# Attention ahead of two routed layers: the order of the background work, of two subtractions and of the q loads

## The chip, the cores and the metric

The kernel runs on one core of a Trainium2 chip. The time is device microseconds of one execution. The kernel before took 952.51 us as the median of three runs (949.66 to 957.09). One further execution was recorded by the hardware profiler; it took 954.63 us, and its span from the first to the last instruction is 952.9 us.

## The reference

Attention over 8 batches, 8 heads, 576 positions and 64 features, with K and V averaged over groups of 8 positions (72 pooled rows). Its output is 4608 tokens of 512 features. They pass a layer of 8 experts (each token goes to one), and then a second such layer with a skip gate.

```python
k_p = k.reshape(B, H, Sp, pool, D).mean(axis=3)
v_p = v.reshape(B, H, Sp, pool, D).mean(axis=3)
scores = scale * np.matmul(q, k_p.transpose(0, 1, 3, 2))
attn = softmax(scores)                       # maximum subtracted first
x = np.matmul(attn, v_p)                     # tokens: (B*S, H*D) = (4608, 512)
# layer 1: top-1 of 8 experts, chosen by logits = x @ w_gate + bias[modality]
out[mask] = gate_w[mask, None] * (np.maximum(x[mask] @ w1[e], 0) @ w2[e])
# layer 2: only rows with x @ w_skip > 0; top-1 again; those rows get x + y
y[mask] = np.maximum(xc[mask] @ w1[e], 0) @ w2[e]
```

## The kernel before

**Attention** works through 36 columns of 128 tokens (c = 0 to 35, `NC`), software-pipelined over three columns (`LAG` = 3). In one turn of the loop at L565, `emit_S` (L299) multiplies scores into the PSUM tile `ps_s` (L310), VectorE (DVE) takes their maximum `mx` (L316), and what stands in the list `late` follows on DVE. `emit_eT` turns the exponentials of the column before (L357), `emit_exp` subtracts the maximum by a matmul (L336, which waits for `mx`) and ScalarE (ACT) takes the exponential `ec` (L340). `emit_AV` (L364) multiplies the column three back with V (L377), and the generator `after_AV` divides on DVE: `rec` (L398, L400), `lg` (L402), `x` (L405), and in the next column the logits `LG` (L409). The finished x goes out to `xd` through SyncE's queue SP (L417, L423).

**Loads and preparation.** SP issues every load in program order. `next_q` loads a unit of q (256 tokens, `q_sb`, L141), `next_kv` the raw K and V (`kt` L121, `v` L132). Eight rows are added by GpSimd (POOL) in a tree of three additions, `pool_rows` (L181 to L183), or by one DVE reduction (L176). `split_q` copies q on ACT (`qs`, L167), `prep_k` transposes the sums (L239) and copies them on ACT into `KB` (L244), `prep_v1` transposes V's sums (L255).

**Background.** The routing of layer 1 starts within attention. Its steps are generators in a queue; `bg.tick()` takes `bg.pace` steps of the first one. `route` finds each token's expert and its rank by a scan (`rt_i` L868, `carry` L872, two matmuls into `R` at L883 and L884) for columns 0 to 8, 9 to 17, 18 to 26 (from c = 12, 21, 30) and 27 to 35 (after the loop). `route_places` writes, per column, two 128x128 tables `OB` (L912) on POOL, for the third group on POOL and DVE in turn. `early_pick` chooses the expert that is worked on first: `count` rounds `carry` into `rc_cb` (L920), multiplies it by ones into `R` (L924), and `er_most`, `er_s` follow (L955, L957). `early_fill` counts a second time for block 1, `early_places` works out `er_oa` (L1013), and `early_slots` turns `er_oa` and `OB` into row numbers by 54 small matmuls into `W0` (L1028) and `rs_lo`, `rs_v` on DVE (L1047, L1049).

**Start of layer 1.** From c = 30 `prepare_first` splits the first weights into a high part (`w1h`, ACT) and a low part (`w1l`, DVE, L1328); at c = 32 and 33 it transposes the gathered tokens into `ps_x` (L1356) and splits these too (`xh` ACT, `xl` DVE, L1360). From c = 35 `gemm1_early` runs one of eight parts f0 to f7 of the first GEMM-1 (L1408, 12 matmuls each; `hh` on ACT L1412, `hl` on DVE L1413), and behind f7 GEMM-2 (L1461) opens the layers proper, which take the rest of the span.

The PSUM tiles `ps_k`, `ps_v`, `ps_g` (attention), `R`, `W0` and `ps_x` share one single buffer (`ps_m`): each waits until the reader of the one before it is done. While `bg.hold` is set, whoever wants that buffer first runs the background on until the flag is cleared (`bg.settle`).

Of the kernel before, what the change touches and what calls it, by code (L numbers as in the profile page):

```python
# [9 lines left out]
F32 = mybir.dt.float32  # L10
# [45 lines left out]
def attention(tc, g, q, k, v, mid, w_gate, bias, const, moe):  # L56
# [4 lines left out]
    with ExitStack() as ctx:  # L61
# [243 lines left out]
        def emit_S(c, then=lambda: None):  # L305
# [18 lines left out]
            next(av)  # L324
            bg.tick()
            bg.tick()
            s_t[c] = ps, mx, av
# [38 lines left out]
        def emit_AV(c):  # L366
# [14 lines left out]
            av = av_t[c] = after_AV(c, ps)  # L381
            next(av)
            bg.tick()
            next(av)
            bg.tick()
            next(av)

# [177 lines left out]
        for c in range(NC + LAG):  # L565
            if c < NC:
                next_q(cols[c][0] + (5 if c == 2 else 4))
                next_kv(c)
                next_q(cols[c][0] + 5)
            if c in (22, 32, 36):  # L570
                bg.pace = 1 if c == 32 else 2
            if 4 <= c < NC - 1:
                emit_S(c, lambda: emit_qT(c + 2))
            elif c < 4:
                if c > 0:
                    emit_S(c)
                    emit_eT(c - 1)
                    emit_exp(c)
                emit_qT(c + 2)
            elif c == NC - 1:  # L580
                emit_S(c, moe.gemm1_early)
            if 4 <= c < NC:
# [40 lines left out]
            if c in route_at:  # L623
# [4 lines left out]
                if c0 == 9:  # L628
                    bg.add(early_places(tc, g, g.r1, 18, 0, 2, sm))
                bg.add(route_places(tc, g, g.r1, c0, n, nc.gpsimd, nc.vector if c0 == 18 else None))  # L630
                if c0 == 18:
                    bg.add(early_fill(tc, g, g.r1, 512, sm, ps_m))
                    bg.add(early_places(tc, g, g.r1, 27, 2, 2, sm))
                    bg.add(early_slots(tc, g, g.r1, 27, g.r1.gidx0[:, 2:4], sm, ps_m))
                    bg.add(moe.gather_second())
# [7 lines left out]
            if c == NC - 3:  # L643
                qs.close()
                moe.open_second()
            moe.prepare_first(c, sm, ps_q, ps_m)
        for _ in av_t.pop(NC - 1):
# [268 lines left out]

def count(tc, g, r, sp, pp, wait):
    nc = tc.nc
# [5 lines left out]
    nc.tensor.matmul(N, lhsT=g.ones, rhs=cb, start=True, stop=True)  # L924
    g.bg.hold = True
    for _ in range(wait):
# [21 lines left out]
def early_pick(tc, g, r, sp, pp, wait=4, fill=None):  # L948

    V = tc.nc.vector  # L950
    N = yield from count(tc, g, r, sp, pp, wait)
    most = sp.tile([128, 1], F32, tag="er_most", name="er_most", bufs=1)
# [17 lines left out]
def early_fill(tc, g, r, n, sp, pp, wait=4):  # L970
    V = tc.nc.vector
    N = yield from count(tc, g, r, sp, pp, wait)
    s = sp.tile([128, E], F32, tag="er_s", name="er_s", bufs=1)
# [203 lines left out]
class Moe:  # L1177
# [146 lines left out]

    def split_w1(self, f, eng=None):
        raw = self.w1r[f // 2][:, :, 128 * (f % 2):128 * (f % 2) + 128]
        self.nc.scalar.copy(self.w1h[f], raw)  # L1327
        (eng or self.nc.vector).tensor_tensor(self.w1l[f], raw, self.w1h[f].bitcast(F32),  # L1328
                                              ALU.subtract)

# [21 lines left out]

    def xT(self, i, t, ps):
        nc = self.nc
        for k in range(4):
# [3 lines left out]
        nc.scalar.copy(hi, ps)  # L1359
        nc.vector.tensor_tensor(self.xl[i % 2][:, :, 128 * t:128 * t + 128], ps, hi.bitcast(F32),  # L1360
                                ALU.subtract)

# [123 lines left out]

    def prepare_first(self, c, sm, ps_q, ps_m):
        self.ps_q = ps_q
        for f in {30: (0,), 31: (1,), 32: (2,), 33: (3,), 34: (4,), 35: (5,), 36: (6,), 37: (7,)}.get(c, ()):
            self.split_w1(f)  # L1490
        if c in (32, 33):
            self.g.bg.settle()
            self.xT(0, c - 32, ps_m.tile([128, 4, 128], F32, tag="m", name="ps_x"))
        if c == 36:
# [594 lines left out]
```

## Time and profile before

| | profiled execution |
|---|---|
| time, span | 954.63 us, 952.9 us |
| TensorE matmul (PE) | 897.7 us busy, 94% of the span |
| weight load (PEld) | 803.9 us, 84% |
| DVE | 689.6 us, 72% |
| POOL | 518.7 us, 54% |
| ACT | 373.4 us, 39% |
| mean granted TensorE clock | 0.978 |

PE is the engine that is busy nearly always, so what it waits for is what the span is made of. The granted clock is the share of the full 2.4 GHz that TensorE was given; at half of it a matmul takes twice as long. In the page's 40 slices PE is busy 8 or 9 tenths of each of the first nine, up to 214 us, and nearly always 9 beyond. Attention and the start of layer 1 fill the first 216 us; the change acts there.

### The profile page before, as it was taken

The numbers are of one execution on the slowest core, as the hardware profiler recorded it, in microseconds if no ns is written. First come the engines' busy times: TensorE is split into PE (matmuls) and PEld (weight loads), VectorE is DVE, ScalarE is ACT, GpSimd is POOL, SyncE is SP. The second block draws the span as 40 slices with busy tenths as digits, with TensorE's granted clock in tenths as the row PEclk, the third lists the DMA queues.
The fourth block names the chain that finished last, engine by engine and source line by source line (L and its number), as shares of the span: only waits on it lengthen the run. The fifth ranks groups of instructions, "written<-read, shape, count | busy, mean of one in ns | idle before, by whom it ended". The sixth has DMA issues, their size and how long they took to land. (4 is left out here: it accounts for less than half of the span.)

```text
span 952.9 us, 19141 instructions
## 1 busy us (share of the span) xinstructions
PE 897.7 (94%) x6239; PEld 803.9 (84%) x6239; DVE 689.6 (72%) x1826; ACT 373.4 (39%) x735; POOL 518.7 (54%) x766
## 2 busy tenths in 40 slices
PE   8899999889999999998999989999889999999994
PEld 6788888888899999996999879999778988979983
DVE  5477787776787788889877898877665667577564
ACT  3456565544122222242222422213403556565554
POOL 5764698404246647666766657575543443445443
PEclk9799999999999999999999999999989999999998
DMA  9999765513211212341224421227114673671441
GB/s 229 223 260 259 223 196 167 185 63 120 72 57 58 95 38 65 125 171 66 74 81 134 174 78 63 74 79 244 60 60 146 216 226 122 203 238 36 128 140 42
DMA packets 86136, 126.02 MB, mean 132 GB/s; under 512 B 13192, under 2 KB 50104, under 8 KB 85866
## 3 DMA queue, kind: packets, MB, share of 16 engines
q1 hardware_dynamic: 75386, 96.68, 32.8%
q0 software_dynamic: 10608, 27.67, 9.5%
q8 instruction: 62, 1.02, 0.4%
q14 instruction: 80, 0.66, 0.2%
HBM read 184.18 MB, written 39.50 MB: 235 GB/s over the span
## 5 line engine op out<-in xcount | busy, mean ns | idle before, releaser
L1408 PE MATMUL ps_g<-xh,w1h 128*128 128x256 f32 x896 | 255.9, 286 | 2.0 <-DVE g_su L1391 1.2
L1408 PE MATMUL ps_g<-xl,w1h 128*128 128x256 f32 x896 | 253.6, 283 | 2.2 <-DVE xl L1360 2.2
L1408 PE MATMUL ps_g<-xh,w1l 128*128 128x256 f32 x896 | 253.0, 282 | 0.0
L1742 DVE CUSTOM_DVE_ANT_0 junk<-x,W 128x512 bf16<-128x512 f32 x324 | 228.2, 704 | 18.7 <-DVEq L1338 6.3
L1461 PE MATMUL ps_g<-w2h,hl 128*128 128x512 f32 x464 | 185.4, 399 | 7.0 <-DVE hl L1413 7.0
L1461 PE MATMUL ps_g<-w2h,hh 128*128 128x512 f32 x464 | 191.1, 412 | 0.7 <-DVE rs_v L1049 0.5
L1461 PE MATMUL ps_g<-w2l,hh 128*128 128x512 f32 x464 | 184.4, 397 | 0.0
L1408 PEld LDWEIGHTS ps_g<-xh,w1h 128*128 128x128 f32 x896 | 170.0, 190 | 8.0 <-issue 1.6
L1408 PEld LDWEIGHTS ps_g<-xl,w1h 128*128 128x128 f32 x896 | 169.2, 189 | 3.9 <-DVE xl L1360 3.0
L1408 PEld LDWEIGHTS ps_g<-xh,w1l 128*128 128x128 f32 x896 | 169.2, 189 | 0.0
L1412 ACT ACTIVATE hh<-ps_g 128x512 fp32r<-128x512 f32 (+1 forms) x116 | 67.6, 583 | 245.6 <-PE ps_g L1408 238.7
L912 POOL TENSOR_SCALAR OB<-iota,BB,pay 128x128 bf16<-128x128 bf16 x126 | 110.7, 887 | 22.4 <-DVE BB L900 19.0
L1413 DVE SCALAR_TENSOR_TENSOR hl<-ps_g,hh 128x512 fp32r<-128x512 f32 (+1 forms) x116 | 77.6, 669 | 62.0 <-ACT hh L1412 35.5
L1461 PEld LDWEIGHTS ps_g<-w2h,hl 128*128 128x128 f32 x464 | 88.0, 190 | 30.5 <-DVE hl L1413 8.3
L1461 PEld LDWEIGHTS ps_g<-w2h,hh 128*128 128x128 f32 x464 | 88.3, 190 | 20.5 <-issue 1.9
L1461 PEld LDWEIGHTS ps_g<-w2l,hh 128*128 128x128 f32 x464 | 88.4, 190 | 16.6
L1328 POOL TENSOR_TENSOR w1l<-w1r,w1h 128x512 fp32r<-128x512 f32 x39 | 50.5, 1314 | 63.1 <-ACT w1h L1327 62.8
L1350 DVE TENSOR_TENSOR w2l<-w2r,w2h 128x512 fp32r<-128x512 f32 x112 | 74.9, 706 | 8.2 <-ACT w2h L1349 4.8
L1708 POOL DMA_INDIRECT out_dram<-x,dsi x38 | 48.1, 1265 | 44.7 <-ACTq L1343 11.6
L1327 ACT CAST w1h<-w1r 128x512 fp32r<-128x512 f32 x120 | 68.3, 620 | 0.4 <-ACT hh L1412 0.4
L1349 ACT CAST w2h<-w2r 128x512 fp32r<-128x512 f32 x112 | 63.9, 616 | 4.0 <-DVE gidxf L1052 2.5
L1320 POOL DMA_INDIRECT xg<-xd,gidx x38 | 45.1, 1188 | 32.8 <-DVE rs_lo L1171 15.7
(295 smaller groups left out, 1393.9 us busy)
## 6 DMA issues: line engine op xcount, KB each, us to landing
w1r<-in_moe_w_dram SPq DMA_DIRECT2D x128, 512.0 KB
w2r<-in_moe_w_dram SPq DMA_DIRECT2D x128, 512.0 KB
x2s<-x SPq DMA_DIRECT2D x19, 522.0 KB
v<-in_v_dram SPq DMA_DIRECT2D x48, 192.0 KB
xd<-x SPq DMA_DIRECT2D x16, 520.0 KB
q_sb<-in_q_dram SPq DMA_DIRECT2D x16, 512.0 KB
kt<-in_k_dram SPq DMA_DIRECT2D x32, 144.0 KB
x2s<-OBx SPq DMA_DIRECT2D x16, 261.0 KB
```

The costliest lines, as they stand in the source:

```text
L912: e.tensor_scalar(g.ob(c)[:, i, :], g.iota, r.BB[:, c:c + 1], r.pay[:, i, c:c + 1], ALU.is_equal, ALU.mult)
L1320: self.nc.gpsimd.indirect_dma_start(out=self.xg[i % 2][:, t, 0:w], out_offset=None, in_=src, in_offset=bass.IndirectOffsetOnAxis(ap=gidx[: ...
L1327: self.nc.scalar.copy(self.w1h[f], raw)
L1328: (eng or self.nc.vector).tensor_tensor(self.w1l[f], raw, self.w1h[f].bitcast(F32), ALU.subtract)
L1349: self.nc.scalar.copy(self.w2h[f], raw)
L1350: (eng or self.nc.vector).tensor_tensor(self.w2l[f], raw, self.w2h[f].bitcast(F32), ALU.subtract)
L1408: nc.tensor.matmul(out, lhsT=a[f][:, k, :], rhs=b[:, k, :], start=(n == 0), stop=(n == 11))
L1412: nc.scalar.activation(out=hh, in_=whole, func=ACTF.Relu)
L1413: nc.vector.scalar_tensor_tensor(hl, in0=whole, scalar=0.0, in1=hh.bitcast(F32), op0=ALU.max, op1=ALU.subtract)
L1461: nc.tensor.matmul(ps, lhsT=a[f][:, tt], rhs=b[f], start=(n == 0), stop=(n == 23))
L1708: self.nc.gpsimd.indirect_dma_start(out=self.out, out_offset=bass.IndirectOffsetOnAxis(ap=self.dsi[i % 2][:, t:t + 1], axis=0), in_=self.x ...
L1742: self.nc.vector.tensor_tensor_reduce(out=self.junk, in0=self.x2[i % 2][:, t, 0:DM], in1=self.W9[:, e, :], scale=1.0, scalar=0.0, op0=ALU. ...
```

## The change

Seven edits, all to the order of things; no arithmetic is added or removed, but for three small copies:

1. `emit_AV` takes no background steps between the divisions of its column; `emit_S` takes four behind the maximum instead of two (with the one after `emit_exp` and the one ahead of the AV steps it is six per column as before).
2. From c = 2 on, q is loaded five units ahead (before: four, and five at c = 2), so that its load stands ahead of the column's K and V in SP's queue.
3. At c = 35 the first part of GEMM-1 is emitted behind all of `emit_S`, where it stood between the scores and the maximum.
4. The pace of the background is 2 at c = 34 and 35 and 3 from c = 36 (before: 1 and 2).
5. The third group's `route_places` runs in turn with `early_fill` and `early_places`, where these came behind it.
6. In `early_pick` and `early_fill` ACT copies the count out of PSUM (`rc_N`), and the background is not held.
7. The subtractions `w1l` (c = 30 to 34) and `xl` (c = 32, 33) go into `late`, that is behind the maximum of the next column.

```diff
@@ -322,8 +322,8 @@
             bg.tick()
             av = av_t.pop(c - LAG - 1, idle())
             next(av)
-            bg.tick()
-            bg.tick()
+            for _ in range(4):
+                bg.tick()
             s_t[c] = ps, mx, av
 
         late = []
@@ -379,11 +379,8 @@
                                      rhs=VB[b % NR][:, j].rearrange("p i w -> p (i w)"),
                                      start=(j % 3 == 0), stop=(j % 3 == 2), skip_group_check=True)
             av = av_t[c] = after_AV(c, ps)
-            next(av)
-            bg.tick()
-            next(av)
-            bg.tick()
-            next(av)
+            for _ in range(3):
+                next(av)
 
         def after_AV(c, ps):
             u, r = cols[c]
@@ -564,11 +561,10 @@
         route_at = {12: (0, 9), 21: (9, 9), 30: (18, 9)}
         for c in range(NC + LAG):
             if c < NC:
-                next_q(cols[c][0] + (5 if c == 2 else 4))
+                next_q(cols[c][0] + (5 if c > 1 else 4))
                 next_kv(c)
                 next_q(cols[c][0] + 5)
-            if c in (22, 32, 36):
-                bg.pace = 1 if c == 32 else 2
+            bg.pace = {22: 2, 32: 1, 34: 2, 36: 3}.get(c, bg.pace)
             if 4 <= c < NC - 1:
                 emit_S(c, lambda: emit_qT(c + 2))
             elif c < 4:
@@ -578,7 +574,8 @@
                     emit_exp(c)
                 emit_qT(c + 2)
             elif c == NC - 1:
-                emit_S(c, moe.gemm1_early)
+                emit_S(c)
+                moe.gemm1_early()
             if 4 <= c < NC:
                 emit_eT(c - 1)
                 emit_exp(c)
@@ -627,10 +624,12 @@
                              early_pick(tc, g, g.r1, sm, ps_m, 7) if c0 == 9 else (), lag))
                 if c0 == 9:
                     bg.add(early_places(tc, g, g.r1, 18, 0, 2, sm))
-                bg.add(route_places(tc, g, g.r1, c0, n, nc.gpsimd, nc.vector if c0 == 18 else None))
+                places = route_places(tc, g, g.r1, c0, n, nc.gpsimd, nc.vector if c0 == 18 else None)
+                if c0 < 18:
+                    bg.add(places)
                 if c0 == 18:
-                    bg.add(early_fill(tc, g, g.r1, 512, sm, ps_m))
-                    bg.add(early_places(tc, g, g.r1, 27, 2, 2, sm))
+                    bg.add(together(places, chain(early_fill(tc, g, g.r1, 512, sm, ps_m),
+                                                  early_places(tc, g, g.r1, 27, 2, 2, sm))))
                     bg.add(early_slots(tc, g, g.r1, 27, g.r1.gidx0[:, 2:4], sm, ps_m))
                     bg.add(moe.gather_second())
             if c == 27:
@@ -643,7 +642,7 @@
             if c == NC - 3:
                 qs.close()
                 moe.open_second()
-            moe.prepare_first(c, sm, ps_q, ps_m)
+            moe.prepare_first(c, sm, ps_q, ps_m, late if c < NC - 1 else None)
         for _ in av_t.pop(NC - 1):
             pass
         g.pm.pool = ps_m
@@ -914,7 +913,7 @@
         yield
 
 
-def count(tc, g, r, sp, pp, wait):
+def count(tc, g, r, sp, pp, wait, copy=False):
     nc = tc.nc
     cb = sp.tile([128, E], BF16, tag="rc_cb", name="rc_cb", bufs=1)
     nc.vector.tensor_copy(cb, r.carry)
@@ -922,7 +921,11 @@
         yield
     N = pp.tile([128, E], F32, tag="m", name="R")
     nc.tensor.matmul(N, lhsT=g.ones, rhs=cb, start=True, stop=True)
-    g.bg.hold = True
+    if copy:
+        ps, N = N, sp.tile([128, E], F32, tag="rc_N", name="rc_N", bufs=1)
+        nc.scalar.copy(N, ps)
+    else:
+        g.bg.hold = True
     for _ in range(wait):
         yield
     return N
@@ -948,7 +951,7 @@
 def early_pick(tc, g, r, sp, pp, wait=4, fill=None):
 
     V = tc.nc.vector
-    N = yield from count(tc, g, r, sp, pp, wait)
+    N = yield from count(tc, g, r, sp, pp, wait, True)
     most = sp.tile([128, 1], F32, tag="er_most", name="er_most", bufs=1)
     mx = sp.tile([128, 1], F32, tag="er_mx", name="er_mx", bufs=1)
     s = sp.tile([128, E], F32, tag="er_s", name="er_s", bufs=1)
@@ -969,7 +972,7 @@
 
 def early_fill(tc, g, r, n, sp, pp, wait=4):
     V = tc.nc.vector
-    N = yield from count(tc, g, r, sp, pp, wait)
+    N = yield from count(tc, g, r, sp, pp, wait, True)
     s = sp.tile([128, E], F32, tag="er_s", name="er_s", bufs=1)
     f = sp.tile([128, 1], F32, tag="er_most", name="er_most", bufs=1)
     V.tensor_tensor(s, N, r.star, ALU.mult)
@@ -1322,11 +1325,12 @@
                 in_offset=bass.IndirectOffsetOnAxis(ap=gidx[:, c + t:c + t + 1], axis=0),
                 bounds_check=src.shape[0] - 1, oob_is_err=False)
 
-    def split_w1(self, f, eng=None):
+    def split_w1(self, f, eng=None, late=None):
         raw = self.w1r[f // 2][:, :, 128 * (f % 2):128 * (f % 2) + 128]
         self.nc.scalar.copy(self.w1h[f], raw)
-        (eng or self.nc.vector).tensor_tensor(self.w1l[f], raw, self.w1h[f].bitcast(F32),
-                                              ALU.subtract)
+        low = partial((eng or self.nc.vector).tensor_tensor, self.w1l[f], raw,
+                      self.w1h[f].bitcast(F32), ALU.subtract)
+        low() if late is None else late.append(low)
 
     def load_split(self, i):
         ET = mybir.EngineType
@@ -1350,15 +1354,16 @@
         (eng or self.nc.vector).tensor_tensor(self.w2l[f], raw, self.w2h[f].bitcast(F32),
                                               ALU.subtract)
 
-    def xT(self, i, t, ps):
+    def xT(self, i, t, ps, late=None):
         nc = self.nc
         for k in range(4):
             nc.tensor.transpose(ps[:, k, :], self.xg[i % 2][:, t, 128 * k:128 * k + 128],
                                 self.g.ident)
         hi = self.xh[i % 2][:, :, 128 * t:128 * t + 128]
         nc.scalar.copy(hi, ps)
-        nc.vector.tensor_tensor(self.xl[i % 2][:, :, 128 * t:128 * t + 128], ps, hi.bitcast(F32),
-                                ALU.subtract)
+        low = partial(nc.vector.tensor_tensor, self.xl[i % 2][:, :, 128 * t:128 * t + 128], ps,
+                      hi.bitcast(F32), ALU.subtract)
+        low() if late is None else late.append(low)
 
     def ps_t(self, name):
         return self.pp.tile([128, 4, 128], F32, tag="tp", name=name, bufs=2)
@@ -1484,13 +1489,13 @@
         self.gathered = True
         yield
 
-    def prepare_first(self, c, sm, ps_q, ps_m):
+    def prepare_first(self, c, sm, ps_q, ps_m, late):
         self.ps_q = ps_q
         for f in {30: (0,), 31: (1,), 32: (2,), 33: (3,), 34: (4,), 35: (5,), 36: (6,), 37: (7,)}.get(c, ()):
-            self.split_w1(f)
+            self.split_w1(f, late=late)
         if c in (32, 33):
             self.g.bg.settle()
-            self.xT(0, c - 32, ps_m.tile([128, 4, 128], F32, tag="m", name="ps_x"))
+            self.xT(0, c - 32, ps_m.tile([128, 4, 128], F32, tag="m", name="ps_x"), late)
         if c == 36:
             self.gates1(0, sm)
         if c == 37:
```

What this does to the order, at three places. First SP's queue, where the loads of K's second tile (`kt`, 16 of them), the unit of q needed at column 8, the store `xd` and V stand; line numbers above 395 are up to 5 apart in the two kernels.

```order
 L121 DMA kt<-in_k_dram 36x512 x4
 L121 DMA kt<-in_k_dram 72x512 x4
+L141 DMA q_sb<-in_q_dram 128x8x128
 L121 DMA kt<-in_k_dram 36x512 x4
 L121 DMA kt<-in_k_dram 72x512 x4
+L414 DMA xd<-x 128x1040
 L141 DMA q_sb<-in_q_dram 128x8x128
-L417 DMA xd<-x 128x1040
+L132 DMA v<-in_v_dram 96x512 x6
```

The q load has moved ahead of the second eight of K's 16 loads.

Second DVE at columns 9 and 10, where the background is the token numbers (`qi`, `ti`, `th`, `pay`). Before:

```order
L316 TENSOR_REDUCE mx<-ps_s 128x8
L810 TENSOR_SCALAR qi<-pi 128x1
L409 TENSOR_REDUCE LG<-lg 128x8
L812 CAST qf<-qi 128x1
L814 TENSOR_SCALAR ti<-tm,qf 128x4
L817 TENSOR_SCALAR th<-ti 128x36
L398 TENSOR_SCALAR rec<-ps_av 128x8
L819 CAST pay_666<-th 128x36
L400 RECIPROCAL rec<-rec 128x8
L821 TENSOR_SCALAR ti<-ti 128x36
L402 TENSOR_TENSOR lg<-ps_av,rec 128x64
```

With the change:

```order
L811 CAST qf<-qi 128x1
L813 TENSOR_SCALAR ti<-tm,qf 128x4
L816 TENSOR_SCALAR th<-ti 128x36
L818 CAST pay_666<-th 128x36
L820 TENSOR_SCALAR ti<-ti 128x36
L395 TENSOR_SCALAR rec<-ps_av 128x8
L397 RECIPROCAL rec<-rec 128x8
```

The steps that stood between the divisions of a column stand ahead of them.

Third PE and DVE at column 34. PE before, with what each instruction waits for:

```order
L310 MATMUL ps_s<-KB_129,qt 128x144 [waits Activation_49]
L310 MATMUL ps_s<-KB_129,qt 128x144 x3
L357 MATMUL ps_et<-ident,ec 96x128 x6
L336 MATMUL ps_s<-mx,nident 128x288 [waits DVE_49]
L336 MATMUL ps_s<-mx,nident 128x288
```

PE with the change, and DVE below it:

```order
L310 MATMUL ps_s<-KB_129,qt 128x144 [waits Activation_49]
L310 MATMUL ps_s<-KB_129,qt 128x144 x3
L923 LDWEIGHTS ones [waits DVE_49]
L923 MATMUL R<-rc_cb,ones 128x8 [waits PE_49]
L357 MATMUL ps_et<-ident,ec 96x128 x6
L336 MATMUL ps_s<-mx,nident 128x288 x2
```

```order
L402 TENSOR_TENSOR x<-ps_av,rec 128x512
L316 TENSOR_REDUCE mx<-ps_s 128x8
L320 TENSOR_TENSOR w1l_2150<-w1r_2147,w1h_2149 128x512
L320 TENSOR_TENSOR xl_2144<-ps_x,xh_2143 128x4x128
L406 TENSOR_REDUCE LG<-lg 128x8
```

The second count's matmul `R`, which stood four parts of GEMM-1 further on, now stands behind the scores of column 34 and ahead of the transposes L357. It takes the buffer that `ps_x` held, so it waits for the `xl` that reads `ps_x`, and that stands behind `mx` and `w1l` (both subtractions carry the line of the loop over `late`, L320). `W0`'s 54 matmuls have moved from behind f7 to between f4 and f5, and in the first GEMM-2 the routing's `R` from behind 18 matmuls to behind 12. POOL's order is the same.

## Rows read from the trace of the kernel before

**Rows 1.** ACT's timeline at column 8: start us, us, instruction, [idle before <- releaser].

```profile
59.27 1.04 ACT L167 COPY qs<-q_sb 128x1024 f32<-128x1024 f32 x1 [3.22 <-DMA q_sb<-in_q_dram]
60.22 1.36 ACT L244 COPY KB<-ps_k 64x288 f32<-64x288 f32 x4
```

**Rows 2.** SP's timeline: the DMA issues ahead of that copy.

```profile
43.85 10.16 SPq L121 DMA_DIRECT2D kt<-in_k_dram  x16
54.77 0.39 SPq L141 DMA_DIRECT2D q_sb<-in_q_dram  x1
```

**Rows 3.** PE's timeline, columns 8 to 10.

```profile
61.68 0.44 PE L255 MATMUL ps_v<-ident,v 96*128 96x96 f32 x3 [0.94 <-POOL VB L260]
63.49 1.84 PE L310 MATMUL ps_s<-KB,qt 128*128 128x144 f32 x8 [1.36 <-ACT ec L340]
...
73.31 0.51 PE L336 MATMUL ps_s<-mx,nident 128*128 128x288 f32 x2 [1.46 <-DVE mx L316]
```

**Rows 4.** Windows: stretch, length, busy of PE, PEld, DVE, ACT, POOL; granted clock, DMA.

```profile
60.00:64.00 4.00, 1.70 (x13) 1.33 (x13) 1.19 (x4) 3.85 (x11) 3.92 (x3) 1.00 1.13 269
64.00:68.00 4.00, 4.00 (x23) 3.94 (x22) 2.56 (x6) 1.09 (x2) 3.84 (x4) 0.57 1.05 318
140.00:144.00 4.00, 2.39 (x18) 1.92 (x16) 4.00 (x5) 1.75 (x3) 3.92 (x2) 1.00 0.02 4
144.00:148.00 4.00, 3.26 (x25) 2.57 (x26) 2.34 (x10) 2.57 (x7) 3.77 (x5) 0.74 0.68 198
440.00:444.00 4.00, 2.10 (x10) 1.47 (x10) 3.89 (x11) 0.00 (x0) 3.53 (x5) 1.00 0.00 0
444.00:448.00 4.00, 3.99 (x17) 3.28 (x18) 3.71 (x13) 1.88 (x4) 1.13 (x7) 1.00 0.08 24
```

**Rows 5.** POOL's timeline at column 9: a step of its tree.

```profile
65.52 2.35 POOL L181 TENSOR_TENSOR t<-kt 108x1024 f32<-108x1024 f32 x1
```

**Rows 6.** DVE's timeline at column 9: a background step.

```profile
66.47 1.42 DVE L814 TENSOR_SCALAR ti<-tm,qf 128x4 int32<-128x4 f32 x1
```

**Rows 7.** PE's timeline at column 25.

```profile
144.74 0.71 PE L239 MATMUL ps_k<-ident,k 108*128 108x108 f32 x4 [1.50 <-DVE er_s L957]
```

**Rows 8.** The weight load's timeline at the same place.

```profile
144.71 0.54 PEld L239 LDWEIGHTS ps_k<-ident,k 108*128 108x128 f32 x4 [1.69 <-POOL t L182]
```

**Rows 9.** PE's waits from 168 to 196 us: us in all, times, longest.

```profile
PE ps_s L336 <- DVE mx L316: 3.7, 5, 1.1
```

**Rows 10.** PE's timeline, columns 34 and 35.

```profile
184.27 1.15 PE L310 MATMUL ps_s<-KB,qt 128*128 128x144 f32 x8
...
193.56 0.51 PE L336 MATMUL ps_s<-mx,nident 128*128 128x288 f32 x2 [0.94 <-DVE mx L316]
```

**Rows 11.** DVE's timeline at columns 32 and 34.

```profile
175.35 0.68 DVE L1328 TENSOR_TENSOR w1l<-w1r,w1h 128x512 fp32r<-128x512 f32 x1
...
185.21 0.68 DVE L1328 TENSOR_TENSOR w1l<-w1r,w1h 128x512 fp32r<-128x512 f32 x1
185.81 0.68 DVE L1360 TENSOR_TENSOR xl<-ps_x,xh 128x512 fp32r<-128x512 f32 x1
186.41 0.75 DVE L316 TENSOR_REDUCE mx<-ps_s 128x8 fp32r<-128x576 f32 x1
```

**Rows 12.** POOL's timeline, columns 33 to 35.

```profile
182.38 6.50 POOL L912 TENSOR_SCALAR OB<-iota,BB,pay 128x128 bf16<-128x128 bf16 x8 [8.71 <-DVE BB L900]
```

**Rows 13.** PE's waits from 196 to 225 us.

```profile
PE R L924 <- DVE rc_cb L920: 0.9, 1, 0.9
PE W L1028 <- DVE er_oa L1013: 0.7, 1, 0.7
PE R L884 <- DVE rt_i L868: 0.6, 1, 0.6
PE ps_g L1461 <- DVE rs_v L1049: 0.5, 1, 0.5
PE ps_g L1408 <- DVE hl L1413: 0.5, 1, 0.5
```

## The prediction

> **What bounds the kernel now.** I read the page first: PE is busy 94% of the span and the clock is at 0.978 of full speed, so an edit of the order can only give back time in which PE waits, or in which it runs at half clock after waiting. Then I read PE's waits and its timeline within attention, where the change acts, and behind each wait the engine that ended it. Four places matter.
>
> At columns 8 to 10, ACT stands 3.22 us for a unit of q [rows 1]. SP issued that load at 54.77, behind 16 loads of K that take 10.16 us to issue [rows 2]; the copy started at 59.27, 4.5 later. The copies into `KB` stand behind it on ACT and end at 61.58 [rows 1]. PE idles 0.94, up to 61.68, because its next transposes need the buffer that those copies read (the row names a POOL instruction, but what ends at the right moment is the copy), then 1.36 for the late `ec`, and at column 10 another 1.46 for `mx` [rows 3]. After that thinner stretch the granted clock is 0.57 for 4 us [rows 4]: 0.43 x 4 = 1.7 us lost.
>
> At column 25 PE waits 1.50, by the row for `er_s`, the step that frees `ps_m` [rows 7]. At columns 31 to 35 the waits for `mx` are 3.7 in all [rows 9]: DVE does `w1l` and `xl` first, 0.60 from start to start, and `mx` after them [rows 11]. From there to GEMM-2 PE waits for the second count, for `hl`, for `er_oa` and for `rs_v`, and within GEMM-2 for the routing's scan [rows 13].
>
> **The change part by part.**
>
> *q ahead of K and V.* The load moves ahead of 8 of the 16 K loads, so it is issued near 43.85 + 10.16/2 = 48.9, lands by the same 4.5 near 53.4, and is wanted at 59.27 - 3.22 = 56.05. The stop on ACT goes, with 2.6 to spare. The eight K loads behind it come about 0.4 later each by q's issue (0.39), 2 us later if its 512 KB hold them up as long as K's own take; POOL wants them at 65.52 [rows 5], and K's last issue ended at 54.0, so this is covered. The two waits (0.94, 1.36) and the half clock (1.7) go: 4.0 us. The third, 1.46, is less sure: the background's steps now stand ahead of `rec`, and such a step, `ti`, ended at 67.89, together with POOL's tree step at 67.87 [rows 5, 6], though it has 4 columns to write. If it is held so again, the chain to `mx` is as late as before; if it passes, 5.5 us go in all. I take -4.7; the bounds are 0 (q lands no earlier) and -5.5.
>
> *Background steps out of the divisions.* Six steps per column remain. At column 14 a few short steps of the scan move ahead of `rec`; at the other columns such steps fill time in which DVE waits for AV. I take 0, with bounds of about half a wait like those of [rows 3], -0.5 and +0.5.
>
> *Column 25.* The count's copy frees `ps_m` before `er_s`. But the weight load of the same transposes puts its 1.69 down to POOL's tree [rows 8], which the change does not move. So 0; the wait is only renamed. The bound is -1.5, and with the half clock behind it (0.26 x 4 = 1.0 [rows 4]) and 0.5 for the same in AV, -3.0.
>
> *Lows behind the maxima.* Of the 3.7, column 35 has 0.94 [rows 9, 10], the columns before it 2.76. In columns 31 to 33 `mx` no longer stands behind `w1l` and `xl`; I leave 0.65 for column 32, where the third group's scan now stands ahead of `rec`. Column 34 gets a new wait. The second count's `R` stands behind the scores and waits for `xl`, which now stands behind `mx` and `w1l`. Scores begin; `mx` can begin 1.25 later, takes 0.67 to the next start, `w1l` and `xl` 0.60 each and some delay [rows 10, 11]: `R` 3.2 us after the scores began, and PE's own scores were done 0.98 after it. So PE stands 2.2, where it stood 1.1 [rows 9]; queued behind `R` are the six transposes L357, L336 and, on ACT, the exponential. New 0.65 + 2.2 against 2.76: +0.1.
>
> By the Trainium skill (SBUF — State Buffer, section "SBUF: two separate sides") a DVE instruction with two inputs in SBUF and a GpSimd instruction that reads SBUF exclude one another for their whole length. `w1l` has two such inputs, so beside POOL's `OB` this would lengthen column 34's wait by up to one `OB`, an estimate of 0.8 us. The trace speaks against it here: `w1l` took 0.68 at 185.21, amid eight `OB` of 6.50 us [rows 11, 12], and the same 0.68 at 175.35, when POOL had been idle for 8.71.
>
> *Column 35.* The first part of GEMM-1 comes behind `emit_S`, so `mx` no longer waits for `hl`: -0.94 [rows 10]; bounds 0 and -0.94.
>
> *Second count.* Its matmul stood between two parts of GEMM-1 and waited 0.9 [rows 13]. That goes, as its new place is priced in column 34: -0.9.
>
> *W0.* Its 54 matmuls move from behind f7 to between f4 and f5. The waits for `hl` (0.5), `er_oa` (0.7) and `rs_v` (0.5) go [rows 13]: -1.7. But GEMM-2 now opens right behind f7, and its first matmul waits for the last `hl`, some 1.0 after PE's last GEMM-1 matmul, by the nearest row, where `mx` stood behind the same pair `hh`, `hl` (0.94 [rows 10]). Net -0.7; bounds 0 and -1.7.
>
> *Routing in GEMM-2.* `R` comes 6 matmuls earlier, but the scan starts earlier too, behind fewer subtractions: of the 0.6 for `rt_i` [rows 13] I take half, -0.3; bounds +0.3 and -0.6.
>
> The sum is -4.7 + 0.1 - 0.94 - 0.9 - 0.7 - 0.3 = -7.4.
>
> **The clock at column 34.** PE now stands 2.2 us in one piece there. Of the stretches with as little work in 4 us, the one with 1.70 busy was followed by 0.57, one with 2.39 by 0.74, one with 2.10 by 1.00 [rows 4]. Two of three fell; I take a fall, at the price of the nearest by work, 0.43 x 4 = +1.7. Bounds 0 and, as a rival, much more.
>
> So -5.7: the profiled 954.63 would become 948.9. That run stood 2.1 above the median of the runs, 952.51; against the median I forecast 946.8.
>
> **Rivals.**
> - *q lands no earlier.* The DMA engines are busy throughout behind that load (a DMA share of 1.13 and 1.05 in [rows 4]), and K's bytes must pass in any case. Then the 4.7 stays: -1.0, 951.5. For it: the busy queue; against it: SP's order decides what is sent first. 15%.
> - *Column 25's wait goes with its half clock.* If `er_s` was the true releaser, -3.0 more: 943.8. 12%, since the weight load's row names POOL.
> - *All of the first gain and no fall of the clock at column 34.* -0.8 and -1.7 more: 944.3. 15%.
> - *The change slows the kernel: the clock falls at column 34 and stays.* The new 2.2 us wait is followed by GEMM-1 parts with waits between them. Each us at half clock costs 0.5 us, against a gain of 7.4; so it decides from 7.4 / 0.5 = 14.8 us on at half speed. The stretches seen lost the clock for about 4 us [rows 4]. If it held from 187 to GEMM-2 at 216, 29 us, it would cost 14.5: +7.1, 959.6. By the Trainium skill (TensorE: Matmul & The Clock Gate, section "HAM oscillation — how this bites in real kernels") gaps between bursts can keep the clock switching; no stretch of this trace shows it for so long. 5%.
>
> **How the numbers follow.** The forecast's own case has 53%. The range takes the rivals at 943.8, 944.3 and 951.5, and the bounds of the unknown terms around them, some 3 us downward and 1 upward: 941 to 952.5; outside it stand the slow rival and some of the ends. A change under 1% (9.5 us) can't be told from none. Faster than 943.0 needs two of the favourable cases at once, or one and a low draw of the runs, which spread by 7 us before: 0.18. Slower than 962.0 needs the clock rival beyond its price: 0.04. Between: 0.78.
>
> **What would show it.** In the profile of the changed kernel: no DMA wait on ACT before `qs` near 56; no waits of PE around 61 and 63, and no clock under 1 in the 4 us behind; at 73 minus the gain, either a wait for `mx` with `ti` ending beside a POOL step, or none. At column 25 the same 1.5 before L239, now put down to POOL. At column 34 a wait of `R` of about 2.2 for `xl` and a clock under 1 behind it; none before L336 at columns 31, 33 and 35. Between f4 and GEMM-2 one wait of about 1.0 where there were three. A wait for q that remains, a column 34 without the wait of `R`, or one whose clock stays down beyond 4 us, would make the prediction wrong.

## The result, and the profile after

The changed kernel takes 944.14 us (median of 7 runs, 942.10 to 947.06), the kernel before 953.07 (7 runs, 949.66 to 957.09): ratio 0.9906, interval 0.9886 to 0.9926. That is 8.9 us faster, inside the range of 941 to 952.5 and 2.7 below the 946.8 that was forecast. The profiled execution has a span of 942.4 us; before it was 952.9.

One naming error of the prediction first: the scan's steps that it puts at column 14 stand in the trace of the kernel before ahead of the L336 at 104.38 us, which is column 17. Two of the expectations below carry the same error; column 17 is said in the text.

**Columns 8 to 10.** The rows that answer to [rows 1, 2], ACT's timeline and SP's:

```profile
56.19 1.05 ACT L167 COPY qs<-q_sb 128x1024 f32<-128x1024 f32 x1
57.14 1.37 ACT L244 COPY KB<-ps_k 64x288 f32<-64x288 f32 x4
```

```profile
51.04 0.39 SPq L141 DMA_DIRECT2D q_sb<-in_q_dram  x1
51.53 4.79 SPq L121 DMA_DIRECT2D kt<-in_k_dram  x8
```

The load is issued at 51.04 (54.77 before) and ACT copies it without a wait. PE, answering to [rows 3], and the windows, answering to the first two of [rows 4]:

```profile
60.84 0.41 PE L255 MATMUL ps_v<-ident,v 96*128 96x96 f32 x3
61.08 1.17 PE L310 MATMUL ps_s<-KB,qt 128*128 128x144 f32 x8
...
67.49 0.51 PE L336 MATMUL ps_s<-mx,nident 128*128 128x288 f32 x2
```

```profile
60.00:64.00 4.00, 4.00 (x37) 3.99 (x36) 2.79 (x11) 2.42 (x7) 3.92 (x3) 1.00 1.07 282
64.00:68.00 4.00, 4.00 (x37) 3.99 (x37) 3.67 (x9) 2.68 (x7) 3.92 (x3) 1.00 1.06 335
96.00:100.00 4.00, 2.09 (x18) 1.83 (x17) 3.93 (x8) 1.74 (x3) 1.87 (x2) 0.98 0.88 218
100.00:104.00 4.00, 4.00 (x22) 3.98 (x22) 1.66 (x7) 0.87 (x4) 0.00 (x0) 0.60 1.01 320
180.00:184.00 4.00, 2.03 (x18) 2.04 (x19) 2.85 (x6) 1.28 (x3) 4.00 (x7) 1.00 1.02 333
184.00:188.00 4.00, 4.00 (x41) 3.65 (x40) 3.23 (x12) 1.31 (x5) 1.12 (x2) 1.00 0.56 217
```

None of the three waits is left, and the clock is full. The other four windows are read below: a clock of 0.60 behind column 17, and a full clock behind column 34 although PE was busy only 2.03 of 4 us there.

**Columns 17, 25 and 34**, PE's timeline:

```profile
99.04 0.51 PE L336 MATMUL ps_s<-mx,nident 128*128 128x288 f32 x2 [1.91 <-DVE mx L316]
...
140.58 0.49 PE L239 MATMUL ps_k<-ident,k 108*128 108x108 f32 x2 [1.62 <-POOL k L183]
...
181.97 0.18 PE L923 MATMUL R<-rc_cb,ones 128*128 128x8 bf16 x1 [2.18 <-DVE xl L320]
```

The first stands at column 17. The second is [rows 7] again, 1.62 instead of 1.50, now put down to POOL's tree. The third is the new wait. DVE ahead of it:

```profile
179.82 0.76 DVE L316 TENSOR_REDUCE mx<-ps_s 128x8 fp32r<-128x576 f32 x1 [0.17 <-PE ps_s L310]
180.50 0.81 DVE L320 TENSOR_TENSOR w1l<-w1r,w1h 128x512 fp32r<-128x512 f32 x1
181.23 0.68 DVE L320 TENSOR_TENSOR xl<-ps_x,xh 128x512 fp32r<-128x512 f32 x1
```

`xl` ends at 181.91 and `R` starts at 181.97. The waits of PE from 160 to 225 us (total, times, longest), answering to [rows 9, 13]:

```profile
PE R L923 <- DVE xl L320: 2.2, 1, 2.2
PE ps_g L1466 <- DVE hl L1418: 1.2, 1, 1.2
PE ps_s L336 <- DVE mx L316: 1.0, 1, 1.0
PE ps_g L1413 <- DVE hl L1418: 0.6, 1, 0.6
PE R L883 <- DVE rt_i L867: 0.4, 1, 0.4
```

**Where the 10.5 us of the two spans came from**, read at the same instruction of both traces: columns 8 to 10, -6.1 (and +0.25 from the first columns); columns 17 and 18, +1.4; 19 to 30, 0.0; 31 to 35, -1.3; from there to GEMM-2, -1.1; from GEMM-2's start to the 61st group of three of its matmuls, -1.2; all the rest of the layers, -2.3. In that last part PE has the same matmuls in the same order in all fourteen profiles, and it differs as much between profiles that have the change.

### The profile page after: what moved, and what is told of

It is laid out like the page before. It is cut to its first block, busy times and chain, and to the rows that moved or that the text cites. A ratio compares the mean times of both kernels' runs of the same rounds, so it can differ in the third digit from the quotient of the medians.

```text
span 942.4 us, 19143 instructions
## 1 busy us (share of the span) xinstructions
PE 889.7 (94%) x6239; PEld 800.6 (85%) x6239; DVE 690.7 (73%) x1826; ACT 373.4 (40%) x738; POOL 516.5 (55%) x766
## 3 DMA queue, kind: packets, MB, share of 16 engines
q8 instruction: 62, 1.02, 0.4%
```

## The experiments

The table gives the start of L336 (the subtraction of the maximum) at some columns and of the first GEMM-2 matmul, in us after the profiled execution of the kernel before; below each other, one execution each. The first columns alone differ by up to 1 us between executions, so differences within a row are what counts. The last column is the span behind GEMM-2's start.

| | col. 7 | 10 | 16 | 18 | 26 | 30 | 35 | GEMM-2 | behind |
|---|---|---|---|---|---|---|---|---|---|
| before | 0 | 0 | 0 | 0 | 0 | 0 | 0 | 0 | 736.9 |
| changed | 0.25 | -5.82 | -5.83 | -4.47 | -4.43 | -4.50 | -5.82 | -6.93 | 733.3 |
| q_only | 0.93 | -2.93 | -1.45 | -1.47 | -3.00 | -3.02 | -2.87 | -2.89 | 739.8 |
| all_but_q | -0.20 | -0.50 | -0.51 | 0.88 | 0.94 | 0.87 | 1.23 | 0.15 | 736.9 |
| all_but_steps | 0.16 | -3.71 | -3.71 | -1.17 | -2.14 | -2.17 | -4.71 | -2.62 | 735.6 |
| all_but_lows | 0.00 | -6.07 | -6.08 | -4.70 | -4.64 | -4.71 | -5.48 | -6.56 | 736.6 |
| q_tokens_later | 0.06 | -6.02 | -6.02 | -6.95 | -6.87 | -6.21 | -6.22 | -6.21 | 736.8 |
| count_later | -0.59 | -6.67 | -6.67 | -6.95 | -6.93 | -6.95 | -9.09 | -8.80 | 735.7 |
| scan_later | 1.06 | -5.02 | -5.03 | -6.92 | -4.95 | -4.75 | -4.40 | -5.50 | 734.1 |
| fill_behind | 0.92 | -5.16 | -5.06 | -5.36 | -5.52 | -5.32 | -8.56 | -7.43 | 734.6 |
| k_tile_later | -0.44 | -6.52 | -6.52 | -5.15 | -4.96 | -5.03 | -6.33 | -7.43 | 734.6 |
| best | 0.04 | -6.03 | -6.04 | -7.93 | -8.51 | -8.32 | -11.57 | -9.37 | 733.9 |
| changed_again | 0.85 | -5.22 | -5.23 | -5.51 | -5.33 | -5.05 | -6.36 | -7.46 | 733.6 |
| all_but_copy | -0.32 | -6.40 | -6.40 | -5.04 | -5.01 | -5.07 | -6.38 | -7.49 | 734.5 |

**The q loads alone**, and **all edits but the q loads**:

```diff
-                next_q(cols[c][0] + (5 if c == 2 else 4))
+                next_q(cols[c][0] + (5 if c > 1 else 4))
```

> The kernel before with one edit: q loaded five units ahead from c = 2 on. Theory A (the q load alone makes the gain at columns 8 to 10): ACT stops no longer for q, PE reaches L336 of column 10 5.9 us earlier than before (73.31 there, near 67.4 here), the clock stays full behind 64 us; time near 947, ratio 0.994. Theory B (part of that gain comes from the background steps no longer standing between a column's divisions): a wait of about 1.5 for mx is left at column 10, 4.4 us gained there, time near 948.5. Either way columns 14, 25, 31 to 39 and GEMM-2 as in the kernel before.

> The changed kernel with q loaded four units ahead again. Theory A: ACT stops about 3 us for q at column 8, PE loses 0.9 and 1.4 there and about 2 at half clock, 73 us at column 10 as in the kernel before; later gains stay (3.5 to 4.5 us): time near 949, ratio 0.996. Theory B: L336 of column 10 comes about 1.5 earlier than before, time near 947.5.

Ratios to the kernel before: 0.9966 (0.9947 to 0.9985) and 0.9985 (0.9959 to 1.001). With the q loads alone PE gains 3.9 from column 7 to column 10, not 6.1, and theory B holds: a wait for `mx` is left. DVE in that run:

```profile
65.83 0.17 DVE L398 TENSOR_SCALAR rec<-ps_av 128x8 f32<-128x8 f32 x1 [1.19 <-PE ps_av L377]
65.92 0.70 DVE L819 CAST pay<-th 128x36 f32<-128x36 int32 x1
66.54 0.19 DVE L400 RECIPROCAL rec<-rec 128x8 f32<-128x8 f32 x1
66.65 2.28 DVE L821 TENSOR_SCALAR ti<-ti 128x36 int32<-128x36 int32 x1
68.85 0.21 DVE L402 TENSOR_TENSOR lg<-ps_av,rec 128x64 f32<-128x64 f32 x1
```

```profile
66.54 2.36 POOL L181 TENSOR_TENSOR t<-kt 108x1024 f32<-108x1024 f32 x1
```

```profile
70.38 0.51 PE L336 MATMUL ps_s<-mx,nident 128*128 128x288 f32 x2 [1.97 <-DVE mx L316]
```

`ti`, which took 0.17 in the changed kernel, took 2.28 and ended at 68.93, with POOL's tree step at 68.90. It stands between `rec` and `lg`, so `lg`, `x`, `mx` and PE wait. The granted clock then fell to 0.86 and 0.71 in the windows from 68 to 76 us, which took 1.5 more. Without the q loads, the steps' new place brings 0.3 at column 10, as theory A had it, not the 1.5 of theory B: ACT stops 4.80 us for q, PE waits 2.52 (its row names no releaser; the copies into `KB` end 0.1 earlier) and 1.37 for what is queued behind the q copy, and those hide the rest. The later gains that were expected in this run did not stay either: the clock fell behind columns 17 and 34. By column 16 the loads alone bring 2.4, the other edits alone 0.3, and all together 6.1.

**The background steps back between the divisions:**

```diff
-            for _ in range(4):
-                bg.tick()
+            bg.tick()
+            bg.tick()
...
-            for _ in range(3):
-                next(av)
+            next(av)
+            bg.tick()
+            next(av)
+            bg.tick()
+            next(av)
```

> The changed kernel with two background steps per column again between the divisions in emit_AV (and two instead of four behind the maximum). Theory A (the longer wait for mx at column 14, 1.91 against 1.58, and the clock of 0.60 behind it come from the scan's steps that now stand ahead of rec): the wait is at most 1.6, the clock stays at 1.0 from 100 to 104, some 1.4 us are gained by column 15, time near 942.5. Rival C (the scan meets POOL's tree at another point because everything comes 6 us earlier): wait and clock fall stay, time 944 as the changed kernel. Theory B of the q runs: a wait of about 1.5 comes back at column 10, time near 945.5.

Ratio 0.9929 (0.9907 to 0.9950). Theory B holds again, with 2.2 of the gain lost at column 10:

```profile
69.59 0.51 PE L336 MATMUL ps_s<-mx,nident 128*128 128x288 f32 x2 [1.96 <-DVE mx L316]
```

At column 17 theory A is right on the wait, 1.56 as in the kernel before, and wrong on the clock: it goes down all the same, to 0.79, 0.50 and 0.86 in the windows from 100 to 112 us, and 3.0 are lost by column 19 (-0.72 there). The kernel before had the same wait and kept a clock of 1.00.

**The token numbers later**, in the run with the q loads alone:

```diff
-            if c == 8:
+            if c == 11:
                 bg.add(setup_tokens(tc, g))
```

> The run with the q loads alone, and the generator of the token numbers (ti, th, pay) added at c = 11 instead of c = 8. With the q loads alone PE still waited 1.97 for mx at column 10 and lost 1.5 more to the clock. Theory E (ti and pay stood between a column's divisions and were held on DVE until a step of POOL's tree ended, so rec and mx came late): without them there the wait at column 10 goes and PE reaches L336 of column 11 5.8 us before the kernel before, as in the changed kernel, and any new wait stands at column 12 or 13, small, since POOL is idle there. Rival F (mx is late at column 10 for another reason, such as DVE's own sums of v or the exponential): the wait of about 2.0 stays at column 10 and PE is 1.5 to 3 us ahead only.

Theory E holds: no wait at column 10, 6.1 ahead of column 7, as in the changed kernel, with the divisions left as they were. The run took 948.39 us, the kernel before, measured beside it, 953.52.

**The lows ahead of the maximum again**, `late` being left out of `prepare_first`'s call:

```diff
-            moe.prepare_first(c, sm, ps_q, ps_m, late if c < NC - 1 else None)
+            moe.prepare_first(c, sm, ps_q, ps_m, None)
```

> The changed kernel with w1l and xl ahead of the maximum again. Theory A: the waits for mx at columns 31 to 33 come back (0.15, 0.5 to 0.7 and 0.7) and the wait of 2.2 before the second count's R at column 34 becomes a wait of 1.1 for mx: PE at L336 of column 34 within 0.5 us of the changed kernel, time 944 to 945. Rival D (the subtractions behind the maximum are most of the gain between columns 30 and 35, and R's wait has another cause): R still waits about 2 us, PE at column 35 is 1.5 us later than in the changed kernel, time near 946.

Ratio 0.9889 (0.9859 to 0.9919), no different from the changed kernel. PE's waits from 160 us on are 0.22, 1.11 and 0.70 for `mx` at columns 31 to 33 and 1.13 for `xl` at column 34, 3.16 in all; in the changed kernel they are 0.97 and 2.18, 3.15. Theory A: the edit mostly moves waits. From column 30 to 35 it brings 0.55 (-1.32 against -0.77), with two waits in place of four; that a wait costs more than its idle time is shown below.

**The second count six steps later**, and **the places ahead of the fill**:

```diff
-                    bg.add(together(places, chain(early_fill(tc, g, g.r1, 512, sm, ps_m),
+                    bg.add(together(places, chain(early_fill(tc, g, g.r1, 512, sm, ps_m, 6),
```

```diff
-                    bg.add(together(places, chain(early_fill(tc, g, g.r1, 512, sm, ps_m),
+                    bg.add(chain(places, chain(early_fill(tc, g, g.r1, 512, sm, ps_m),
```

> The changed kernel with the second count waiting six steps instead of four, so that its matmul R stands behind L336 of column 34 instead of ahead of the transposes. Theory A (R's wait of 2.2 is for the late xl of column 33 and holds the transposes and the exponential behind it): the wait before R falls to about 1 or less, L336 of column 34 comes 0.8 to 1.2 us earlier than in the changed kernel, GEMM-2 starts about 1 us earlier; time near 943.5, ratio to the kernel before 0.989. Rival D (the wait only moves: R waits the rest of xl, and AV behind it): less than 0.4 us at GEMM-2's start.

> The changed kernel with the third group's places ahead of early_fill and early_places again, not in turn with them. Theory A (taking them in turn moved the second count out of GEMM-1, for 1.2, and put the wait of 2.2 into column 34, and left the start of GEMM-2 as it was): no R at column 34, its L336 about 1.2 us earlier than in the changed kernel; a wait of about 0.9 for the count between two parts of GEMM-1; three waits of 1.7 together before GEMM-2 instead of 1.8; GEMM-2's start within 0.6 us of the changed kernel. Rival H (it is the earlier W0 that pays): GEMM-2 starts 1 us or more later than in the changed kernel.

The first has a ratio of 0.9935 (0.9913 to 0.9957); the second took 944.85 us in one run, the kernel before 953.52. The first edit also reads the count two steps later, since `count` lets that many steps pass both ahead of `R` and behind it. With the count behind L336, `R` waits 0.82 and PE gains 0.8 more from column 30 to 35. It is given back at once:

```profile
PE ps_g L1413 <- DVE hl L1418: 2.4, 1, 2.4
```

`W0` has moved on too, from between f4 and f5 to between f6 and f7. f6 needs the buffer that `hl` of f4 reads, and that `hl` is late (`hh` stands on ACT behind the copy of the last column's `LG`); in the changed kernel the 1.49 us of `W0` fill this time. From column 30 to GEMM-2 the changed kernel gains 2.4, this one 1.9: of theory A the shorter wait came, its gain at GEMM-2 did not. With the places ahead, 3.2 are gained up to column 35 and 1.1 lost behind it, in a wait of 1.7 for `er_oa` and a clock of 0.63 and 0.94 beside it: 2.1, against 2.4. So the new order of places and count is worth 0.3 us in these two profiles; theory A. That fall of the clock is up to 1.7 of it (0.37 and 0.06 of 4 us, an estimate), so at a full clock the old order would be ahead.

**The scan one column later:**

```diff
-            eng, lag = (nc.vector, (0, 0)) if c0 == 18 else (nc.gpsimd, (5, 8) if c0 == 0 else (4, 12))
+            eng, lag = (nc.vector, (0, 0)) if c0 == 18 else (nc.gpsimd, (5, 14) if c0 == 0 else (4, 12))
...
-            bg.pace = {22: 2, 32: 1, 34: 2, 36: 3}.get(c, bg.pace)
+            bg.pace = {21: 2, 32: 1, 34: 2, 36: 3}.get(c, bg.pace)
```

> The changed kernel with the first group's scan six steps later (one column), and the background's pace 2 one column earlier, at c = 21, so that the second group keeps its place. Theory E (at column 17 the scan 2.36 and the carry 1.18 are held on DVE until POOL's tree steps end, and rec and mx stand behind them): beside an idle POOL they take 0.3 and 0.2, the wait of 1.9 for mx goes, and with it the clock of 0.60 behind it; PE is 1.9 to 3.3 us ahead of the changed kernel from column 19 on; time near 941.5, ratio 0.987. Rival G (the scan itself takes that long wherever it stands): the wait moves by one column, nothing gained.

Ratio 0.9914 (0.9893 to 0.9935). Theory E: in the changed kernel scan and carry ended with POOL's tree steps, DVE and POOL:

```profile
93.59 2.36 DVE L867 TENSOR_TENSOR_SCAN rt_i<-within,rt_ms 128x72 bf16<-128x72 f32 x1
95.99 1.18 DVE L871 CAST carry<-rt_i 128x8 f32<-128x8 bf16 x1
```

```profile
93.44 2.35 POOL L181 TENSOR_TENSOR t<-kt 108x1024 f32<-108x1024 f32 x1
95.87 1.27 POOL L182 TENSOR_TENSOR t<-t 108x512 f32<-108x512 f32 x1
```

The scan later:

```profile
98.44 0.40 DVE L867 TENSOR_TENSOR_SCAN rt_i<-within,rt_ms 128x72 bf16<-128x72 f32 x1
98.88 1.61 DVE L871 CAST carry<-rt_i 128x8 f32<-128x8 bf16 x1
```

The scan takes 0.40 (the carry still 1.61, beside the next tree step), PE's wait falls from 1.91 to 0.34, and from column 16 to 18 1.9 are gained on the kernel before, where the changed kernel lost 1.4. At column 20, 3.5 are lost for another reason, on ACT and then on PE, and the 941.5 that theory E expected did not come (945.85):

```profile
107.70 1.04 ACT L167 COPY qs<-q_sb 128x1024 f32<-128x1024 f32 x1 [3.90 <-DMA q_sb<-in_q_dram]
```

```profile
110.52 2.28 PE L310 MATMUL ps_s<-KB,qt 128*128 128x144 f32 x8 [1.77 <-ACT ec L340]
```

That is the fault of column 8 at another unit of q, behind eight loads of K's fourth tile. The run with the places ahead of the fill shows it too (3.36 on ACT); the changed kernel shows it in one of its two profiles (2.69). Of the ten profiles with the earlier loads and K's order as it was, six show it and four do not.

**These loads of K later, the version put together, the changed kernel again:**

```diff
-                 ("k", 6), ("k", 7), ("v", 10), ("v", 11), ("k", 8), ("v", 12), ("v", 13), ("k", 9),
+                 ("k", 6), ("k", 7), ("v", 10), ("v", 11), ("v", 12), ("v", 13), ("k", 8), ("k", 9),
```

> The changed kernel with the first half of K's fourth tile (8 loads, used by POOL from 131 us on) issued behind two more V loads, so that it no longer stands in SP's queue ahead of the units of q that ACT wants between 95 and 110 us. In two of the runs of near relatives of the changed kernel ACT stopped 3.4 and 3.9 us there and PE lost about 3.5 with the half clock behind it; in the profiled run of the changed kernel it did not. Theory I (the same fault as at column 8, only that it strikes in some executions): no DMA wait before qs between 90 and 112 us, PE at column 21 as in the best of these runs; the median of the runs 1 to 2 us under the changed kernel of the same visit, the lowest about the same. Rival J (the DMA queues are full there, the bytes of V come first now and q lands as late): the stop stays, in some executions 3 us; no gain.

> Put together from the runs: the changed kernel with the first group's scan one column later and pace 2 from c = 21 (no wait of 1.9 at column 17), the half tile of K later (no late q), and the third group's places ahead of early_fill again (no R at column 34). If the gains add: 2 to 3.5 us at column 17 to 19, 1 on average from q, 0.5 to 1 up to GEMM-2: about 4 us under the changed kernel, ratio to the kernel before near 0.986. If the gains do not add (a wait moved on, as at column 8 with either edit alone): ratio 0.990.

> The changed kernel again, beside the run put together from the others: ratio to the kernel before near 0.9906. Its second profile tells whether the half clock behind column 17, its absence behind column 34 and the fast layers of the first profile belong to the kernel or to that execution: if to the kernel, GEMM-2 starts at 209 and the span behind it is 733; if to the execution, they differ by 1 to 3 us.

Measured side by side: 0.9919 (0.9888 to 0.9950), 0.9879 (0.9853 to 0.9905) and 0.9915 (0.9887 to 0.9944). ACT stops for no unit of q at 105 us in the first two. Theory I also wanted no stop at 95 us, where 2.31 and 1.47 are left (they reach nothing on PE), and a gain of 1 to 2 us, which is not measured: 944.99 against 944.01. With one profile each and four of ten that have no stop at 105 us either, theory I is not shown. The version put together has a median of 942.09 against 944.01 for the changed kernel, and five of its six runs are faster than all six of the changed kernel; the intervals of the two ratios overlap, so 2 us is likely and not certain. The 4 us that were expected if the gains add did not come: 2.2 are given back between column 35 and GEMM-2, where `W0` waits 1.7 for `er_oa` and the clock falls to 0.72 and 0.50.

The second profile of the changed kernel starts GEMM-2 0.5 earlier than the first and takes 733.6 behind it, so these belong to the kernel as far as two profiles tell. The half clock behind column 17 does not: the wait there is 1.93 again, and the clock stays full.

```profile
96.00:100.00 4.00, 2.07 (x20) 1.61 (x17) 3.90 (x8) 2.31 (x3) 2.40 (x3) 1.00 0.95 219
100.00:104.00 4.00, 4.00 (x36) 3.99 (x35) 3.32 (x10) 1.81 (x5) 0.00 (x0) 1.00 0.88 252
```

Behind column 34 the clock is full in both.

**Without the copy of the count** (`if copy:` made false; the count is read out of PSUM and the background held):

> The changed kernel without the copy of the count on ACT (and with the background held until the count is read). Theory A (at column 25 the copy only renames the wait, since POOL's tree ends last): the wait of about 1.6 before L239 stays, PE at column 26 within 0.3 us of the changed kernel. Rival K (the copy frees the buffer and pays): the wait grows, or another appears at column 35 or 36, 0.5 us or more.

Theory A: 1.43 for `er_s` before L239, nothing gained or lost at column 26 (-5.04 before it, -5.01 behind). The run took 944.81 us, the kernel before 953.21.

No run takes back the first part of GEMM-1 behind `emit_S` or the new pace alone; what is said of these two rests on the rows.

## Why the prediction was right

*q and the background's steps (-4.7, bounds 0 and -5.5; measured -6.1).* The mechanism of the load was right: no stop on ACT, both waits and the half clock gone. Its margin was not: the load was issued at 51.04, not 48.9, since the first eight loads of K took 6.69 us and not half of 10.16, and in the profiles where ACT waited for it it had taken 5.2 to 6.0, not 4.5. In the twelve profiles with the earlier load that wait was 0 to 0.64: just in time, not 2.6 to spare. For the third wait the prediction left open whether the steps get past POOL's tree. They don't: `pay` took 1.14 in the changed kernel, from 63.98 to 65.12, beside a tree step that ended at 65.07. But it ran where DVE had nothing else to do, and `rec` followed at 65.16 without harm. So the steps' new place earns 2.2 of the 6.1 (the run without it), and only together with the loads; the forecast held 0.7 for it, half of the third wait. The bound was exceeded by 0.6: 4.3 came where the first two waits and the clock were priced at 4.0, and 1.8 for the third, whose row has 1.46. For L336 the traces show why a wait costs more than the idle time in its row. Column 34 of the kernel before, and below it column 33 of the changed kernel, where nothing is waited for:

```profile
185.25 0.82 PE L357 MATMUL ps_et<-ident,ec 128*96 128x128 f32 x6
187.21 0.51 PE L336 MATMUL ps_s<-mx,nident 128*128 128x288 f32 x2 [1.14 <-DVE mx L316]
```

```profile
175.78 0.82 PE L357 MATMUL ps_et<-ident,ec 128*96 128x128 f32 x6
176.35 0.51 PE L336 MATMUL ps_s<-mx,nident 128*128 128x288 f32 x2
```

Without a wait L336 begins 0.57 behind the first transpose, 0.25 before the end of their row; with it 1.96 behind. So the wait of 1.14 cost 1.39.

*Column 17 (0, within 0.5; measured +1.4).* The wait grew by 0.3 and L336 came 0.5 later, as `rec` stands behind scan and carry (without the steps' new place neither happened), and the clock behind it fell to 0.60. The wait for `rt_rk`, which the prediction did not name, went (0.4). The clock is the part that failed, and only in this execution: in the second profile, with a full clock, the place came to -0.3.

*Column 25 (0).* Right: 1.62, put down to POOL. Its rival at 943.8 falls, although the time came out near it. (The rival took the half clock at 1.0 from one window; the next one, at 0.83, makes it 1.7.)

*Columns 31 to 35 (+0.1 and -0.94; measured -1.3).* The new wait of `R` was 2.18 where 2.2 was said, column 32 kept 0.97 where 0.65 was said, column 35 none. By idle time alone that is 3.69 against 3.15, or -0.5. But where the waits of 0.15, 0.71 and 0.94 at columns 31, 33 and 35 went, PE gained 0.40, 0.95 and 1.21: some 0.25 more each, as above.

*The clock at column 34 (+1.7; measured 0).* Wrong for this execution, and a matter of the execution: with the same wait of 2.18 or 2.19 the clock stayed full in four profiles and fell in two. In the run with the later scan:

```profile
180.00:184.00 4.00, 2.27 (x13) 2.27 (x14) 2.56 (x6) 1.31 (x3) 4.00 (x7) 0.78 0.91 329
184.00:188.00 4.00, 4.00 (x34) 3.65 (x33) 1.89 (x6) 0.90 (x4) 0.88 (x2) 0.79 0.56 219
```

That is 0.43 x 4 = 1.7 us, the price that was taken. The slow rival, a clock that stays down, came nowhere. What came is the third rival, at 944.3 with 15%: all of the first gain, and no fall at column 34. The forecast's own case was right on the waits, but it had a fall of 1.7 at column 34; one of 1.7 came behind column 17 instead. That the two nearly cancel is luck.

*Count and W0 (-0.9 and -0.7; measured -1.1 together).* The count's wait went. At `W0` the three waits of 1.7 became two of 1.8: the last `hl` was waited for 1.24, not 1.0, since three steps of the routing (`rt_mx`, `rt_eq`) stood ahead of it on DVE, and 0.6 for f4's `hl` was left out. The net is 0, one of the bounds.

*Routing in GEMM-2 (-0.3; measured -1.2).* Under-priced: the wait for `M` (0.4) went as well as part of that for `rt_i`, and the next GEMM-1 begins 13.4 to 13.5 us behind GEMM-2's start in nine of the eleven profiles that have most of the change (12.9 and 14.3 in the other two), 14.1 to 14.4 in the three that have not. A third wait, 0.28 for `rs_oa` (L1162) within that GEMM-1, went too.

Of the profiled -10.5 the forecast of -5.7 thus misses 1.7 for a clock that held, 1.4 at columns 8 to 10, 0.9 in GEMM-2 and 0.5 at columns 31 to 35, less 1.4 at column 17, 0.5 at `W0` and 0.3 in the first columns. What remains, 2.3 to 2.5 in the rest of the layers, is not explained: the stretch from the 61st group on took 652.3 in the kernel before and 649.9 in the changed kernel, 649.9 to 653.5 in the eleven profiles with the change or most of it and 651.9 to 654.8 in the three without. The traces show where the two executions differ: in that stretch PE lost 12.7 us to the half clock in the kernel before and 8.3 in the changed kernel (the share of the clock not granted, summed over the stretch), while its waits grew from 17.1 to 19.7. With the change that loss was 5.5 to 12.5, without it 9.8 to 12.7, so it is not shown to come from the change.

## What to carry to other kernels

Price edits that meet in one chain together: here a late load and a blocked step between two divisions hid one another, and the edits brought 2.4 and 0.3 apart and 6.1 together. Put steps that another engine can hold where their own engine is idle, not between two instructions of a chain that is waited for. When a wait is moved, look at what filled it: here `W0` filled the time of a late `hl`, and moved away it left a wait of 2.4. And compare when the same instruction starts, not the idle time alone: the waits at L336 cost 0.25 more than their rows say.

## What the runs showed of the hardware

Small DVE instructions beside POOL's tree ended with its step: `ti` 2.28 with 2.36, `rt_i` 2.36 with 2.35, `carry` 1.18 with 1.27, though they write 128x8 to 128x72 and take 0.17 to 0.40 elsewhere. Not every one did: `qi` (128x1) took 0.14 beside such a step in the changed kernel. By the Trainium skill (SBUF — State Buffer, section "SBUF: two separate sides") the port pair that DVE and GpSimd share is held for the whole instruction of whichever has it first. The first three agree in when they ended, and no row here tells why `qi` passed. `w1l`, with two SBUF inputs, does not: beside POOL's `OB` it took 0.81 instead of 0.68 at column 34, and the `OB` that began within it 0.87 instead of 0.78; in the kernel before, `w1l` at 185.21 took 0.68 and the `OB` that began within it 1.02. They held one another up for 0.1 to 0.2 us, not for an `OB` of 0.8.

The same wait did not fix the clock. Behind the 1.9 us at column 17 it fell in five profiles of this order, to 0.59 to 0.69 in the worse window, and stayed full in three; behind the 2.2 us at column 34 it fell in two of six. A fall cost from 1.5 us (q loads alone, column 10) to 3.0 (steps back, column 17), and it is part of what separates executions of one kernel: the two profiles of the changed kernel are 1.65 apart at column 18 by it, counted from column 7.
